# Two units per run: order of scores, queries, values and projections in an attention block with a gate

## The chip, the core and the metric

The kernel runs on one core of a Trainium2 chip. The metric is the device time of one execution in microseconds (us); lower is better. Five executions of the kernel before took 929.92, 929.92, 930.09, 930.19 and 933.02 us: median 930.09. A profile of one more execution shows where the time goes.

## The reference

```python
def _A_ref(x, k_cache, v_cache, wq, wo):          # 32 heads of 192, 2048 rows
    W = min(4096, max(256, Sk // 4))              # 512: the last 512 keys
    q = (x @ wq) split into heads
    k, v = k_cache[:, :, Sk - W:, :], v_cache[:, :, Sk - W:, :]
    p = softmax(q @ k^T * Dh ** -0.5)
    return (p @ v) joined over heads @ wo

def _B_ref(x, w_gate, w_up, w_down):
    return (sigmoid(x @ w_gate) * (x @ w_up)) @ w_down

xn = layernorm(x)                                  # x: 2048 x 640, bf16
out = x + _A_ref(xn, ...) * silu(_B_ref(xn, ...))
```

The sizes: 2048 rows, width 640, 32 heads with 192 values each, 512 keys per head, 1536 hidden columns in the gated part. Everything comes in and goes out as bf16.

## The kernel before

Two stages follow each other. **Stage one** normalizes x, turns it so that the width lies on the partitions (`xnT`), and computes the gated part into `gate`, in four blocks of 512 rows. Weights come in pieces, issued at lines 158 to 171, mostly on SyncE's queue (SP), the first of the gate weights on ScalarE's (ACT). Row block 0 starts tile by tile (`tile_gates`, L291); the first matmuls need the first weights and the first tiles of x. During block 2 the first group of attention inputs is loaded (L344), during block 3 its keys are turned (L346). At the end the queries of unit 0 are computed with 128-row matmuls (`query_psum`, L358).

**Stage two** is attention and its output projection. Heads come in 8 groups of 4, rows in 4 blocks of 512; one group on one block is a **unit**, 32 in all, numbered u = 4 x group + block. A unit has four kinds of work on TensorE (PE):

- `scores` (L390): eight steps, one for each of two head pairs and four key chunks. A head has 192 columns, cut as 3 x 64, so a step is 6 matmuls of 64 rows, two of them side by side in the two halves of the array, into the two halves of one PSUM bank pair. ScalarE takes the Exp of the 128 x 1024 result (L394) into the tile `E`.
- `queries` for the next unit (L408): six half-steps of 10 matmuls, also of 64 rows, set between the score steps, so that PE has work while ScalarE does the Exp. VectorE (DVE) copies the first element of a half-done sum (L413) and the finished sum (L415).
- `values` (L425): four heads, each 16 matmuls of 128 rows and 193 columns (the last column is the softmax sum); DVE takes the reciprocal and divides (L430, L431) into `o_st`.
- `project` (L445): for each of four row tiles, 12 matmuls of 128 rows of the unit before, added to `acc` by DVE (L458, L460), and written out in the last group (L449 to L456). In group 6 of 0 to 7, GpSimd (POOL) multiplies `acc` by the gate and adds the row of x (L463 to L465).

The loop at line 467 does, for each unit, first its scores with the queries of unit u + 1, and then its values with the projections of unit u - 1. The order on every engine is the order of the program: the scheduling is manual. PSUM is used as four bank pairs, `bank[0]` to `bank[3]`; the numbers in the calls pick one.

The inputs of a group: `wq_sb` (query weights), `k_st` (keys as loaded), `k_perm` (keys permuted by four POOL copies, L112), `kT` (keys turned by eight DMA transposes on SP, L128), `vbuf` (values, four loads), `wo_sb` (output weights). `wq_sb`, `kT`, `vbuf` and `wo_sb` have two buffers each. `load_group` and `load_wo` for the next group are called after the scores of block 1 and issue on POOL's queue; `turn_keys` after those of block 2. After a unit's values, `turn_out` (L437) turns `o_st` into `oT` with four DMA transposes on SP. The last unit has an order of its own (lines 491 to 504).

Of the kernel before, what the change touches and what calls it, by code (L numbers as in the profile page):

```python
# [15 lines left out]
def kernel(  # L16
# [13 lines left out]
    nc = tc.nc  # L30
# [31 lines left out]
    psum = ctx.enter_context(tc.tile_pool(name="psum", bufs=1, space=bass.MemoryType.PSUM))  # L62
    rs = dict(side="right")
    pers = ctx.enter_context(tc.tile_pool(name="pers", bufs=1, **rs))
    load2 = ctx.enter_context(tc.tile_pool(name="load2", bufs=2, **rs))
    load1 = ctx.enter_context(tc.tile_pool(name="load1", bufs=1, **rs))
    qpool = ctx.enter_context(tc.tile_pool(name="qpool", bufs=2, **rs))


    bank = [psum.tile([P, 2, 512], F32, name=f"bank{i}") for i in range(4)]  # L70
# [9 lines left out]

    xnT = pers.tile([P, NB, NCD, TB], BF16, name="xnT")
    gate = pers.tile([P, NT, D], BF16, name="gate")
    vbuf = [pers.tile([P, 4, KC, VP], BF16, name=f"vbuf{i}") for i in range(2)]

    wq_r = A_wq.rearrange("(c p) n -> p c n", p=P)
    wo_r = A_wo.rearrange("(c p) d -> p c d", p=P)
# [3 lines left out]

    grp = {}

    def load_group(g, eng):

        d = grp.setdefault(g, {})
        d["wq"] = load2.tile([P, NCD, GW], BF16, name="wq_sb")
        eng.dma_start(d["wq"][:], wq_r[:, :, g * GW:(g + 1) * GW])
        kst = load1.tile([P, 4, KC, DH], BF16, name="k_st")
        kv = slice(Sk - W, Sk)
        eng.dma_start(  # L100
            kst[:].rearrange("p h j d -> p h (j d)"),
            A_k_cache[0, 4 * g:4 * g + 4, kv, :].rearrange("h (p j) d -> p h (j d)", j=KC),
        )
        d["v"] = vbuf[g % 2]
        for h in range(4):
            eng.dma_start(  # L106
                d["v"][:, h, :, 0:DH],
                A_v_cache[0, 4 * g + h, kv, :].rearrange("(p j) d -> p j d", j=KC),
            )
        kp = load1.tile([P, 2, KC, DJ, P], BF16, name="k_perm")  # L110
        for h in range(4):
            nc.gpsimd.tensor_copy(  # L112
                kp[:, h // 2, :, :, (h % 2) * H2:(h % 2) * H2 + H2],
                kst[:, h, :, :].rearrange("p c (i j) -> p c j i", j=DJ),
            )
        d["kp"] = kp

    def load_wo(g):
        d = grp[g]
        d["wo"] = wo_pool.tile([P, GC, D], BF16, name="wo_sb")  # L120
        nc.gpsimd.dma_start(d["wo"][:], wo_r[:, g * GC:(g + 1) * GC, :])

    def turn_keys(g):
        d = grp[g]
        d["kT"] = load2.tile([P, 2, DJ, W], BF16, name="kT")
        for pr in range(2):
            for c in range(KC):
                nc.sync.dma_start_transpose(  # L128
                    d["kT"][:, pr, :, c * P:(c + 1) * P],
                    d["kp"][:, pr, c, :, :].rearrange("p j i -> p (j i)"),  # L130
                )


    with ExitStack() as bctx:
# [18 lines left out]
        def load_f(eng, w, r, f0, f1, c0=0, c1=NCD):  # L153
            eng.dma_start(w[:, c0:c1, f0 * P:f1 * P], r[:, c0:c1, f0 * P:f1 * P])
# [3 lines left out]
        nc.vector.memset(wg_sb[:, 0, 0:2], 0.0)  # L158
        load_x(0, 1)
        load_x(1, 1)  # L160
        load_f(nc.scalar, wg_sb, wg_r, 0, 4)
        load_f(nc.sync, wu_sb, wu_r, 0, 4, 0, 3)
        load_x(2, 1)
        load_f(nc.sync, wu_sb, wu_r, 0, 4, 3, NCD)
        load_x(3, 1)
# [7 lines left out]
        nc.scalar.activation(junk[:], eps_t[:], AF.Sqrt)  # L173
        nc.gpsimd.memset(mhalf[:], -0.5)
        make_identity(nc, ident[:])
        for i in range(2):
            nc.gpsimd.memset(vbuf[i][:, :, :, DH:DH + 2], 1.0)

        def dummy(n):
            for _ in range(n):  # L180
# [150 lines left out]
        for b in range(1, NB):  # L331
            for f in range(2):
                gated(b, f, k)
                k = (k + 1) % 4
            for q in range(TQ):
                down(b - 1, q, k)
                k = (k + 1) % 4
            if b == 1:
                load_x(3 * TQ, TQ)
            for f in range(2, NF):  # L340
                gated(b, f, k, norm_piece(b + 1, f - 4) if b + 1 < NB and f >= 4 else None)
                k = (k + 1) % 4
            if b == 2:
                load_group(0, nc.sync)  # L344
            if b == 3:
                turn_keys(0)  # L346
        for q in range(TQ):
# [4 lines left out]
        def query_psum(u, n, k, half):  # L352

            g, b = u // NB, u % NB
            wq = grp[g]["wq"]
            col = (n // DJ) * 2 * DH + n % DJ
            for c in range(NCD):
                nc.tensor.matmul(bank[k][:, half, :], lhsT=wq[:, c, col:col + DJ * (P - 1) + 1:DJ],  # L358
                                 rhs=xnT[:, b, c, :], start=(c == 0), stop=(c == NCD - 1))

        qT[0] = qpool.tile([P, 2 * DJ, TB], BF16, name="qT")
        for m in range(DJ):
            for half in range(2):
                query_psum(0, 2 * m + half, k, half)
            nc.vector.tensor_copy(qT[0][:, 2 * m:2 * m + 2, :], bank[k][:])
            k = (k + 1) % 4


    wo_pool = ctx.enter_context(tc.tile_pool(name="wo_pool", bufs=2))
    acc_pool = ctx.enter_context(tc.tile_pool(name="acc_pool", bufs=1))  # L370
    e_pool = ctx.enter_context(tc.tile_pool(name="e_pool", bufs=2))
    o_pool = ctx.enter_context(tc.tile_pool(name="o_pool", bufs=1))
    oT_pool = ctx.enter_context(tc.tile_pool(name="oT_pool", bufs=2))
    small = ctx.enter_context(tc.tile_pool(name="small", bufs=4))
    fin = ctx.enter_context(tc.tile_pool(name="fin", bufs=4))

    acc = acc_pool.tile([P, NT, D], F32, name="acc")
    NU = NG * NB
# [17 lines left out]
    def queries(u, m, k, second):  # L396

        g, b = u // NB, u % NB
        wq = grp[g]["wq"]
        if u not in qT:  # L400
            qT[u] = qpool.tile([P, 2 * DJ, TB], BF16, name="qT")
        for c in range(NCD):
            for i in range(2):
                half = i ^ second
                n = 2 * m + half
                col = (n // DJ) * 2 * DH + n % DJ
                r = slice(i * H2, (i + 1) * H2)
                nc.tensor.matmul(bank[k][:, half, :], lhsT=wq[r, c, col:col + DJ * (P - 1) + 1:DJ],  # L408
                                 rhs=xnT[r, b, c, :], start=(c == 0 and not second),
                                 stop=(c == NCD - 1), skip_group_check=bool(second))  # L410
        if not second:

            nc.vector.tensor_copy(seen[:, m, :], bank[k][:, :, 0])  # L413
        else:
            nc.vector.tensor_copy(qT[u][:, 2 * m:2 * m + 2, :], bank[k][:])  # L415
# [1 line left out]
    o_st = {}  # L417

    def values(u, h, k):
        g = u // NB  # L420
        v, e = grp[g]["v"], E[u, h // 2]
        o4 = wide(k).rearrange("p (q n) -> p q n", q=TQ)
        for q in range(TQ):
            for c in range(KC):
                nc.tensor.matmul(o4[:, q, 0:DH + 1], lhsT=e[:, c, h % 2, q * P:(q + 1) * P],  # L425
                                 rhs=v[:, h, c, 0:DH + 1], start=(c == 0), stop=(c == KC - 1))
        if h == 0:
            o_st[u] = o_pool.tile([P, TQ, GW], BF16, name="o_st")
        rden = small.tile([P, TQ, 1], F32, name="rden")
        nc.vector.reciprocal(rden[:], o4[:, :, DH:DH + 1])  # L430
        nc.vector.tensor_tensor(o_st[u][:, :, h * DH:(h + 1) * DH], o4[:, :, 0:DH],  # L431
                                rden[:].to_broadcast([P, TQ, DH]), ALU.mult)
# [31 lines left out]
            nc.gpsimd.tensor_tensor(acc[:, t, :], acc[:, t, :], gate[:, t, :], ALU.mult)  # L464
            nc.gpsimd.tensor_tensor(acc[:, t, :], acc[:, t, :], x_sb[:], ALU.add)  # L465

    for u in range(NU):
        g, b = u // NB, u % NB
        nxt = u + 1 < NU
        sc = [(pr, c) for pr in range(2) for c in range(KC)]  # L470
        if nxt:
            for i, what in enumerate(((0, 0), (1, 0), (0, 1), (1, 1), (2, 0), None, (2, 1), None)):
                scores(u, *sc[i], i % 2)
                if what is not None:
                    queries(u + 1, what[0], 2 + what[0] % 2, what[1])
        if b == 1 and g + 1 < NG:
            load_group(g + 1, nc.gpsimd)
            load_wo(g + 1)
        if b == 2 and g + 1 < NG:
            turn_keys(g + 1)  # L480
        if nxt:
            order = (3, 2, 0, 1, 3, 2, 0, 1) if u else (3, None, 2, None, 0, None, 1, None)
            for q in range(4):
                values(u, q, order[2 * q])
                if q == 3:
                    turn_out(u)
                if u > 0:
                    project(u - 1, q, order[2 * q + 1], nc.sync)


    u = NU - 1
    for i, k in enumerate((3, 2, 0, 1, 3, 2)):
        scores(u, *sc[i], k)
    project(u - 1, 0, 0, nc.sync)
    scores(u, *sc[6], 1)
    scores(u, *sc[7], 3)
    for h, k in enumerate((2, 0, 1, 3)):
        values(u, h, k)
    turn_out(u)
    for q, k in ((1, 2), (2, 0), (3, 1)):  # L500
        project(u - 1, q, k, nc.sync)
    for q, k in ((0, 3), (1, 2), (2, 0)):
        project(u, q, k, nc.scalar)
    project(u, 3, 1, None)


# [28 lines left out]
```

The softmax here doesn't subtract the row's maximum and nothing guards it: scores larger than these inputs give would overflow.

## Time and profile before

| what | us |
|---|---|
| median of five executions | 930.09 |
| the profiled execution | 930.21 |
| its span in the profile | 928.4 |
| PE busy | 916.9 |
| VectorE busy | 467.6 |
| ScalarE busy | 304.8 |
| POOL busy | 126.5 |
| first score matmul / last unit's first score matmul | 170.57 / 899.49 |
| from one unit to the next, in the steady part | 23.72 |

The times inside the profile count from the start of the span. The span is 1.8 us shorter than the time of the same execution. "PE" is the matmuls, "PEld" the loading of their stationary operands, which overlaps. A line such as L390 is that line of the kernel before. In a timeline, square brackets behind an entry give how long the engine stood idle before it, and what ended that. In the list of DMA issues the columns are the tensor, the queue and kind, the count, the size of one and the median time from issue to landing. The TensorE clock was granted in full nearly throughout (mean 0.999).

### The profile page before, as it was taken

To read this page: it belongs to the slowest core of one execution; us is meant where nothing else is said; L and a number is where in the kernel's file an instruction comes from. 1 tells how busy PE (TensorE), PEld (TensorE's weight loads), DVE (VectorE), ACT (ScalarE), POOL (GpSimd) and SP (SyncE) were. 2 spreads that over 40 slices of the span, in tenths; PEclk is the share of its full clock that TensorE was granted. 3 is DMA by queue.
4 is the path that set the end of the run, shared out by engine and by line. 5 is a ranking of instruction groups with operands and counts; after the bars stand their busy time and mean duration, and the time that the engine had idled before them with its cause. 6 is when DMAs were issued, how large, how long until landed. Compare 5 with 4: busy or idle time off the path is not lost.

```text
span 928.4 us, 18032 instructions
## 1 busy us (share of the span) xinstructions
PE 916.9 (99%) x7954; PEld 545.4 (59%) x8034; DVE 467.6 (50%) x739; ACT 304.8 (33%) x333; POOL 126.5 (14%) x154
## 2 busy tenths in 40 slices
PE   8999999999999999999999999999999999999997
PEld 6445455565666556666556666556666666666665
DVE  5452522455545545445545445544555555445657
ACT  4222222433333333333333333333333333333341
POOL 1000100400010001000200020002000205555000
PEclk9999999999999999999999999999999999999999
DMA  9310420616224423443343433263326234422223
GB/s 320 78 29 1 128 46 1 196 36 145 53 53 78 121 68 61 77 95 94 61 77 62 118 70 78 57 124 69 78 49 131 69 69 76 93 63 64 50 67 102
DMA packets 157823, 76.69 MB, mean 83 GB/s; under 512 B 140800, under 2 KB 151664, under 8 KB 157744
## 3 DMA queue, kind: packets, MB, share of 16 engines
q1 hardware_dynamic: 149264, 45.90, 24.8%
q0 software_dynamic: 7248, 28.38, 10.9%
q8 instruction: 63, 1.03, 0.5%
q10 hardware_dynamic: 1232, 1.25, 0.4%
q14 instruction: 16, 0.13, 0.1%
HBM read 39.45 MB, written 2.62 MB: 45 GB/s over the span
## 4 chain that ended last, share of the span: by engine, by line
PE 97%; DVE 1%; DMA 1%; issue 1%; SPq 0%; ACT 0%; DVEq 0%
PE bank L408 22%; PE bank L445 21%; PE bank L425 19%; PE bank L390 18%; PE bank L241 10%; PE bank L253 6%; PE bank L291 1%; PE bank L358 1%; DMA x_sb<-in_A_x_dram 1%; DVE gate L454 1%; DVE o_sb L449 1%; PE bank L221 0%; SPq L149 0%; ACT xnT L227 0%; DVE st L189 0%
## 5 line engine op out<-in xcount | busy, mean ns | idle before, releaser
L394 ACT ACTIVATE E<-bank 128x1024 bf16<-128x1024 f32 x256 | 257.9, 1023 | 477.4 <-PE bank L390 465.6
L408 PE MATMUL bank<-xnT,wq_sb 64*128 64x512 bf16 x1860 | 231.3, 376 | 0.0
L445 PE MATMUL bank<-wo_sb,oT 128*128 128x128 bf16 (+1 forms) x1473 | 225.2, 296 | 3.3
L390 PE MATMUL bank<-qT,kT 64*128 64x512 bf16 x1536 | 202.1, 376 | 0.0
L425 PE MATMUL bank<-vbuf,E 128*128 128x193 bf16 x2048 | 191.0, 247 | 0.0
L425 PEld LDWEIGHTS <-E 128*128 128x128 bf16 x2048 | 167.8, 98 | 24.2 <-issue 13.6
L415 DVE CAST qT<-bank 128x1024 bf16<-128x1024 f32 x93 | 113.9, 1225 | 132.8 <-PE bank L408 132.8
L445 PEld LDWEIGHTS <-oT 128*128 128x128 bf16 x1536 | 121.3, 98 | 76.6 <-issue 0.4
L408 PEld LDWEIGHTS <-wq_sb 64*128 64x128 bf16 x1860 | 97.0, 100 | 104.8
L390 PEld LDWEIGHTS <-kT 64*128 64x128 bf16 x1536 | 72.9, 94 | 90.1 <-issue 8.8
L431 DVE TENSOR_TENSOR o_st<-bank,rden 128x768 bf16<-128x768 f32 x128 | 122.5, 957 | 4.8 <-DVE rden L430 0.4
L460 DVE TENSOR_TENSOR acc<-bank,acc 128x640 f32<-128x640 f32 x96 | 79.2, 825 | 44.1 <-PE bank L445 44.1
L413 DVE COPY seen<-bank 128x2 f32<-128x2 f32 x93 | 14.8, 159 | 93.9 <-PE bank L408 93.8
L430 DVE RECIPROCAL rden<-bank 128x4 f32<-128x4 f32 x128 | 23.3, 182 | 71.0 <-PE bank L425 70.8
L241 PE MATMUL bank<-xnT,wg_sb 128*128 128x512 bf16 x216 | 54.5, 379 | 0.2
L241 PE MATMUL bank<-xnT,wu_sb 128*128 128x512 bf16 x215 | 54.4, 379 | 0.3
L253 PE MATMUL bank<-wd_sb,hT 128*128 128x128 bf16 (+1 forms) x376 | 52.4, 297 | 0.4
L247 DVE TENSOR_TENSOR hT<-bank,sig 128x512 bf16<-128x512 f32 x44 | 30.3, 689 | 42.9 <-ACT sig L244 42.9
L244 ACT ACTIVATE sig<-bank 128x512 bf16<-128x512 f32 x44 | 26.3, 597 | 68.4 <-PE bank L241 65.3
L106 POOL DMA_DIRECT2D vbuf<-in_A_v_cache_dram x28 | 20.9, 747 | 184.9 <-PE bank L425 184.9
L253 PEld LDWEIGHTS <-hT 128*128 128x128 bf16 x384 | 29.7, 98 | 23.1
L241 PEld LDWEIGHTS <-wu_sb 128*128 128x128 bf16 x220 | 21.5, 98 | 26.0
(51 smaller groups left out, 275.8 us busy)
## 6 DMA issues: line engine op xcount, KB each, us to landing
wo_sb<-in_A_wo_dram POOLq DMA_DIRECT2D x8, 960.0 KB, 7.4
wq_sb<-in_A_wq_dram POOLq DMA_DIRECT2D x7, 960.0 KB, 6.3
k_st<-in_A_k_cache_dram POOLq DMA_DIRECT2D x7, 768.0 KB, 8.3
vbuf<-in_A_v_cache_dram POOLq DMA_DIRECT2D x28, 192.0 KB, 3.0
row<-in_A_x_dram POOLq DMA_DIRECT2D x16, 160.0 KB, 2.7
oT<-o_st SPq DMA_TRANSPOSE x128, 2.6
x_sb<-in_A_x_dram SPq DMA_DIRECT2D x3, 640.0 KB, 10.3
wd_sb<-in_B_w_down_dram SPq DMA_DIRECT2D x1, 1920.0 KB, 13.8
```

Source lines behind the costliest of these rows:

```text
L241: nc.tensor.matmul(bank[k][:, half, 0:r1 - r0], lhsT=w[:, c, f * P:(f + 1) * P], rhs=xnT[:, b, c, r0:r1], start=(c == 0), stop=(c == NCD - 1))
L244: nc.scalar.activation(sig[:, 0:r1 - r0], bank[k][:, 0, 0:r1 - r0], AF.Sigmoid)
L247: nc.vector.tensor_tensor(hT[b][:, f, r0:r1], bank[k][:, 1, 0:r1 - r0], sig[:, 0:r1 - r0], ALU.mult)
L253: nc.tensor.matmul(wide(k)[:, d0:d1], lhsT=hT[b][:, f, q * P:(q + 1) * P], rhs=wd_sb[:, f, d0:d1], start=(f == 0), stop=(f == NF - 1))
L390: nc.tensor.matmul(bank[k][:, i, :], lhsT=kT[r, pr, j, c * P:(c + 1) * P], rhs=q[r, pr * DJ + j, :], start=(j == 0), stop=(j == DJ - 1))
L394: nc.scalar.activation(E[u, pr][:, c, :, :], bank[k][:], AF.Exp, scale=scale_qk)
L408: nc.tensor.matmul(bank[k][:, half, :], lhsT=wq[r, c, col:col + DJ * (P - 1) + 1:DJ], rhs=xnT[r, b, c, :], start=(c == 0 and not second), ...
L415: nc.vector.tensor_copy(qT[u][:, 2 * m:2 * m + 2, :], bank[k][:])
L425: nc.tensor.matmul(o4[:, q, 0:DH + 1], lhsT=e[:, c, h % 2, q * P:(q + 1) * P], rhs=v[:, h, c, 0:DH + 1], start=(c == 0), stop=(c == KC - 1))
L431: nc.vector.tensor_tensor(o_st[u][:, :, h * DH:(h + 1) * DH], o4[:, :, 0:DH], rden[:].to_broadcast([P, TQ, DH]), ALU.mult)
L445: nc.tensor.matmul(wide(k)[:, d0:d1], lhsT=oT[u][:, cc, q * P:(q + 1) * P], rhs=wo[:, cc, d0:d1], start=(cc == 0), stop=(cc == GC - 1))
L460: nc.vector.tensor_tensor(acc[:, t, :], wide(k)[:, 0:D], acc[:, t, :], ALU.add)
```

## The change

The order of stage two is changed from one unit at a time to two. The loop goes over pairs (u0, u0 + 1): the scores of both units come first, with the queries of u0 + 2 and u0 + 3 between them; then the values of both, with the projections of u0 - 2 and u0 - 1. The last pair has an order of its own: 16 score steps with the eight projections of the pair before among them, then the values of both units, then their projections. Unit 1's queries are computed ahead of the loop, with unit 0's.

The buffers of a group become single: one each for `wq_sb`, `kT`, `vbuf` and `wo_sb`. In their place there are four `qT`, four `E`, and two `o_st`; the rows of x at the end get two buffers instead of four. The keys are loaded in two halves through one `k_st` of half the size, with two POOL copies after each. The output weights of the last group go into the place of the query weights, and all output weights are issued on SP instead of POOL. The calls that load and turn move to the first point at which the single buffer is free: query weights and keys after the scores of the first pair of a group, the turn of the keys after the scores of the second pair, values after that pair's values, output weights after the values and projections of the next group's first pair.

At the very start the first gate weights are cut in two, three of five chunks on ACT and two on SP, and the first three chunks of the up weights move from SP to ACT.

The core of the diff:

```diff
-    load2 = ctx.enter_context(tc.tile_pool(name="load2", bufs=2, **rs))
     load1 = ctx.enter_context(tc.tile_pool(name="load1", bufs=1, **rs))
-    qpool = ctx.enter_context(tc.tile_pool(name="qpool", bufs=2, **rs))
+    qpool = ctx.enter_context(tc.tile_pool(name="qpool", bufs=4, **rs))
...
-    vbuf = [pers.tile([P, 4, KC, VP], BF16, name=f"vbuf{i}") for i in range(2)]
+    vbuf = pers.tile([P, 4, KC, VP], BF16, name="vbuf")
...
+    def load_keys(g, eng):
+        kp = load1.tile([P, 2, KC, DJ, P], BF16, name="k_perm")
+        for pr in range(2):
+            kst = load1.tile([P, 2, KC, DH], BF16, name="k_st")
+            h0 = 4 * g + 2 * pr
+            eng.dma_start(
+                kst[:].rearrange("p h j d -> p h (j d)"),
+                A_k_cache[0, h0:h0 + 2, kv, :].rearrange("h (p j) d -> p h (j d)", j=KC),
+            )
+            for i in range(2):
+                nc.gpsimd.tensor_copy(
+                    kp[:, pr, :, :, i * H2:(i + 1) * H2],
+                    kst[:, i, :, :].rearrange("p c (i j) -> p c j i", j=DJ),
+                )
...
     def load_wo(g):
         d = grp[g]
-        d["wo"] = wo_pool.tile([P, GC, D], BF16, name="wo_sb")
-        nc.gpsimd.dma_start(d["wo"][:], wo_r[:, g * GC:(g + 1) * GC, :])
+        if g < NG - 1:
+            d["wo"] = wo_pool.tile([P, GC, D], BF16, name="wo_sb")
+        else:
+            d["wo"] = load1.tile([P, GC, D], BF16, name="wo_last", tag="wq_sb")
+        nc.sync.dma_start(d["wo"][:], wo_r[:, g * GC:(g + 1) * GC, :])
...
-        load_f(nc.scalar, wg_sb, wg_r, 0, 4)
-        load_f(nc.sync, wu_sb, wu_r, 0, 4, 0, 3)
+        load_f(nc.scalar, wg_sb, wg_r, 0, 4, 0, 3)
+        load_f(nc.sync, wg_sb, wg_r, 0, 4, 3, NCD)
+        load_f(nc.scalar, wu_sb, wu_r, 0, 4, 0, 3)
...
+        ks = iter((1, 2, 3, 0, 3, 1))
+        for u in range(2):
+            qT[u] = qpool.tile([P, 2 * DJ, TB], BF16, name="qT")
+            for m in range(DJ):
+                k = next(ks)
+                for half in range(2):
+                    query_psum(u, 2 * m + half, k, half)
+                nc.vector.tensor_copy(qT[u][:, 2 * m:2 * m + 2, :], bank[k][:])
...
+    order = (2, 3, 0, 1)
+    for u0 in range(0, NU - 2, 2):
+        g, second = u0 // NB, u0 % NB != 0
+        more = g + 1 < NG
+        for u in (u0, u0 + 1):
             for i, what in enumerate(((0, 0), (1, 0), (0, 1), (1, 1), (2, 0), None, (2, 1), None)):
                 scores(u, *sc[i], i % 2)
                 if what is not None:
-                    queries(u + 1, what[0], 2 + what[0] % 2, what[1])
+                    queries(u + 2, what[0], 2 + (what[0] + u) % 2, what[1])
+        if more and not second:
+            load_wq(g + 1, nc.gpsimd)
+            load_keys(g + 1, nc.gpsimd)
+        if more and second:
+            turn_keys(g + 1)
+        if not more:
+            load_wo(g)
+        for u in (u0, u0 + 1):
             for q in range(4):
+                if u0 > 0:
+                    values(u, q, order[2 * q % 4])
+                    project(u - 2, q, order[(2 * q + 1) % 4], nc.sync)
+                else:
+                    values(u, q, order[q])
+            turn_out(u)
+        if more and second:
+            load_values(g + 1, nc.gpsimd)
+        if 0 < g < NG - 1 and not second:
+            load_wo(g)
+
+    u = NU - 2
+    sc = [(v, *s) for v in (u, u + 1) for s in sc]
+    for i in range(6):
+        scores(*sc[i], order[i % 4])
+    for q in range(2):
+        project(u - 2, q, q, nc.sync)
+    for i in range(6, 12):
+        scores(*sc[i], order[(i - 6) % 4])
+    for q in range(2, 4):
+        project(u - 2, q, q - 2, nc.sync)
+    for i in range(12, 16):
+        scores(*sc[i], order[i % 4])
+    for q in range(4):
+        project(u - 1, q, order[q], nc.sync)
+    for v in (u, u + 1):
+        for h in range(4):
+            values(v, h, order[h])
+        turn_out(v)
+    for q in range(4):
+        project(u, q, order[q], nc.sync)
+    for q in range(4):
+        project(u + 1, q, order[q], nc.scalar if q < 3 else None)
```

More of the change, by code (lines that the diff above doesn't have):

```diff
@@ L91, with load_wq @@
     grp = {}
-    def load_group(g, eng):
+    kv = slice(Sk - W, Sk)
+    def load_wq(g, eng):
         d = grp.setdefault(g, {})
-        d["wq"] = load2.tile([P, NCD, GW], BF16, name="wq_sb")
+        d["wq"] = load1.tile([P, NCD, GW], BF16, name="wq_sb")
         eng.dma_start(d["wq"][:], wq_r[:, :, g * GW:(g + 1) * GW])
[L98 to L104, printed above, removed]
+    def load_keys(g, eng):
[12 more added lines that the diff above has]
+                )
+        grp[g]["kp"] = kp
@@ L105, in load_group, with load_values @@
+    def load_values(g, eng):
         for h in range(4):
             eng.dma_start(
-                d["v"][:, h, :, 0:DH],
+                vbuf[:, h, :, 0:DH],
                 A_v_cache[0, 4 * g + h, kv, :].rearrange("(p j) d -> p j d", j=KC),
             )
[L110 to L115, printed above, removed]
@@ L116, in load_group @@
-        d["kp"] = kp
     def load_wo(g):
         d = grp[g]
-        d["wo"] = wo_pool.tile([P, GC, D], BF16, name="wo_sb")
-        nc.gpsimd.dma_start(d["wo"][:], wo_r[:, g * GC:(g + 1) * GC, :])
+        if g < NG - 1:
[3 more added lines that the diff above has]
+        nc.sync.dma_start(d["wo"][:], wo_r[:, g * GC:(g + 1) * GC, :])
     def turn_keys(g):
         d = grp[g]
-        d["kT"] = load2.tile([P, 2, DJ, W], BF16, name="kT")
+        d["kT"] = load1.tile([P, 2, DJ, W], BF16, name="kT")
@@ L175 @@
         make_identity(nc, ident[:])
-        for i in range(2):
-            nc.gpsimd.memset(vbuf[i][:, :, :, DH:DH + 2], 1.0)
+        nc.gpsimd.memset(vbuf[:, :, :, DH:DH + 2], 1.0)
         def dummy(n):
@@ L343 @@
             if b == 2:
-                load_group(0, nc.sync)
+                load_wq(0, nc.sync)
+                load_keys(0, nc.sync)
+                load_values(0, nc.sync)
             if b == 3:
@@ L359, in query_psum @@
                                  rhs=xnT[:, b, c, :], start=(c == 0), stop=(c == NCD - 1))
[L361 to L369, printed above, removed]
+        ks = iter((1, 2, 3, 0, 3, 1))
[6 more added lines that the diff above has]
+                nc.vector.tensor_copy(qT[u][:, 2 * m:2 * m + 2, :], bank[k][:])
+    wo_pool = ctx.enter_context(tc.tile_pool(name="wo_pool", bufs=1))
     acc_pool = ctx.enter_context(tc.tile_pool(name="acc_pool", bufs=1))
-    e_pool = ctx.enter_context(tc.tile_pool(name="e_pool", bufs=2))
-    o_pool = ctx.enter_context(tc.tile_pool(name="o_pool", bufs=1))
+    e_pool = ctx.enter_context(tc.tile_pool(name="e_pool", bufs=4))
+    o_pool = ctx.enter_context(tc.tile_pool(name="o_pool", bufs=2))
     oT_pool = ctx.enter_context(tc.tile_pool(name="oT_pool", bufs=2))
     small = ctx.enter_context(tc.tile_pool(name="small", bufs=4))
-    fin = ctx.enter_context(tc.tile_pool(name="fin", bufs=4))
+    fin = ctx.enter_context(tc.tile_pool(name="fin", bufs=2))
     acc = acc_pool.tile([P, NT, D], F32, name="acc")
@@ L419, in values @@
     def values(u, h, k):
-        g = u // NB
-        v, e = grp[g]["v"], E[u, h // 2]
+        e = E[u, h // 2]
         o4 = wide(k).rearrange("p (q n) -> p q n", q=TQ)
@@ L425, in values @@
                 nc.tensor.matmul(o4[:, q, 0:DH + 1], lhsT=e[:, c, h % 2, q * P:(q + 1) * P],
-                                 rhs=v[:, h, c, 0:DH + 1], start=(c == 0), stop=(c == KC - 1))
+                                 rhs=vbuf[:, h, c, 0:DH + 1], start=(c == 0), stop=(c == KC - 1))
         if h == 0:
@@ L465, in project @@
             nc.gpsimd.tensor_tensor(acc[:, t, :], acc[:, t, :], x_sb[:], ALU.add)
[L467 to L471, printed above, removed]
+    sc = [(pr, c) for pr in range(2) for c in range(KC)]
+    order = (2, 3, 0, 1)
[3 more added lines that the diff above has]
+        for u in (u0, u0 + 1):
             for i, what in enumerate(((0, 0), (1, 0), (0, 1), (1, 1), (2, 0), None, (2, 1), None)):
@@ L474 @@
                 if what is not None:
-                    queries(u + 1, what[0], 2 + what[0] % 2, what[1])
[L476 to L479, printed above, removed]
+                    queries(u + 2, what[0], 2 + (what[0] + u) % 2, what[1])
[3 more added lines that the diff above has]
+        if more and second:
             turn_keys(g + 1)
-        if nxt:
-            order = (3, 2, 0, 1, 3, 2, 0, 1) if u else (3, None, 2, None, 0, None, 1, None)
+        if not more:
+            load_wo(g)
@@ L483 @@
+        for u in (u0, u0 + 1):
             for q in range(4):
[L484 to L504, printed above, removed]
+                if u0 > 0:
[6 more added lines that the diff above has]
+            load_values(g + 1, nc.gpsimd)
```

## The prediction

> **What bounds the kernel.** I read the page's busy table first, then the chain that ended last, then the timeline of one unit in the steady part, and last the waits and the DMA issues.
>
> ```profile
> span 928.4 us, 18032 instructions
> ...
> PE 916.9 (99%) x7954; PEld 545.4 (59%) x8034; DVE 467.6 (50%) x739; ACT 304.8 (33%) x333; POOL 126.5 (14%) x154
> ...
> PE 97%; DVE 1%; DMA 1%; issue 1%; SPq 0%; ACT 0%; DVEq 0%
> ```
>
> PE sets the time: 99% busy and 97% of the chain, with no wait behind it. A transfer or an engine that already hides can give nothing. Only PE's own work, or a gap inside it, can. So I took one unit from the timeline between 500 and 560 us (columns: start, duration, engine, line, operation).
>
> ```profile
> 518.20 1.79 PE L445 MATMUL bank<-wo_sb,oT 128*128 128x512 bf16 x12
> ...
> 519.92 0.33 PEld L390 LDWEIGHTS <-kT 64*128 64x128 bf16 x6 [0.26 <-issue]
> 519.93 0.82 PE L390 MATMUL bank<-qT,kT 64*128 64x512 bf16 x6
> ...
> 528.57 1.46 PE L390 MATMUL bank<-qT,kT 64*128 64x512 bf16 x12
> ...
> 529.42 1.94 ACT L394 ACTIVATE E<-bank 128x1024 bf16<-128x1024 f32 x2 [0.64 <-PE bank L390]
> ...
> 529.87 1.24 PE L408 MATMUL bank<-xnT,wq_sb 64*128 64x512 bf16 x10
> ...
> 530.94 0.81 PE L390 MATMUL bank<-qT,kT 64*128 64x512 bf16 x6
> ...
> 531.68 1.28 PEld L425 LDWEIGHTS <-E 128*128 128x128 bf16 x16 [0.42 <-issue]
> 531.69 1.51 PE L425 MATMUL bank<-vbuf,E 128*128 128x193 bf16 x16
> ```
>
> Starts, not durations, tell the pace, since the matmuls overlap. A score step takes (529.87 - 528.57)/2 = 0.65 us inside the run of two, a query half-step 1.07 (529.87 to 530.94). But the last score step, 530.94 to 531.69, takes 0.75: 0.10 is lost where PE goes from 64-row matmuls to 128-row ones. At the other end a projection takes 1.63 between its neighbours (509.31 to 510.94 in the same view), so 518.20 should end at 519.83, and the next scores start at 519.93: 0.10 to 0.11 lost. The weight loads show it too: both "issue" gaps stand at these two places and nowhere else in the unit. The total agrees: 8 x 0.65 + 6 x 1.07 + 4 x (1.33 + 1.63) = 23.5, and units repeat every 23.72 us.
>
> **Part 1, switches removed.** Before, PE enters the 64-row matmuls 33 times (32 units, and once more in the tail) and leaves them 33 times: 66 switches. After, there are 15 pairs in the loop and 3 runs of scores in the tail: 18 entries and 18 exits, 36 switches. So 15 of each kind go: 15 x 0.10 + 15 x 0.11 = **3.15 us**. It is all on PE's path, so it counts in full. Everything else that PE does stays: scores, values and projections are the same in number; unit 1's queries become 30 matmuls of 128 rows in place of 60 of 64, which take 164.00 to 170.57 us for unit 0 now, 6.5 us, against 6 x 1.07 = 6.4: nothing.
>
> The Trainium skill, "TensorEngine Tiling (Array Packing)", Key Properties, says that changing the tiling mode drains TensorE, which fits the place of the gaps. "TensorE: Matmul & The Clock Gate", Single matmul latency, puts the part of a lone matmul that isn't streaming at 398 cycles of 2.4 GHz, 166 ns; were all of that exposed, 30 switches would be an estimated 5.0 us and the time about 925.0. The row has 0.10 to 0.11, and I go by the row.
>
> **Part 2, the new seams.** Inside a run, unit u+1's first score step follows unit u's last. It writes bank 0, whose last reader is the Exp of step 6. Taking the rows above: the two Exps end at 529.42 + 1.94 = 531.36, and the new step would start at 530.94 + 0.65 = 531.59. Margin 0.23 us; the shortest hand-over to PE in the trace is 0.06 (xn ends at 8.53, PE starts at 8.59), so 0.17 is left and I take zero. If the cover were gone by 0.1, it would cost 15 x 0.1 = 1.5 us. The next step uses bank 1: it starts 1.72 later, at 533.3, and Exp 7 ends at about 532.8. The query banks alternate with the unit, so the last cast (to 532.38) isn't waited for. On the values side values and projection alternate as now, DVE needs 0.18 + 0.96 + 0.82 of each 2.96 us, and four banks rotate. Below zero: the first unit's values without projections end once instead of once per unit; that is 0.1 us at most.
>
> **Part 3, single buffers and moved loads.** A scores run is now 2 x 11.65 = 23.3 us, a values run 23.7 (10.7 in the first pair, 8 x 1.33, which has no projections). Each load has to fit between the last reader and the first user.
>
> ```profile
> wq_sb<-in_A_wq_dram POOLq DMA_DIRECT2D x7, 960.0 KB, 6.3
> k_st<-in_A_k_cache_dram POOLq DMA_DIRECT2D x7, 768.0 KB, 8.3
> ...
> oT<-o_st SPq DMA_TRANSPOSE x128, 2.6
> ...
> kT<-k_perm SPq DMA_TRANSPOSE x64, 2.4
> ```
>
> (The last column is us from issue to landing.)
> - Query weights: free at the end of the scores run, wanted 23.7 + 0.65 us later; they need 0.87 + 6.3, at most 7.4. In the first pair the window is 10.7 + 0.65 = 11.3 against 8.3: the tightest, 3 us of cover, once.
> - Keys: two half loads with POOL's copies between, 2 x (0.78 + 8.2 + 2 x 0.83) = 21.3 us, wanted by SP's transposes 34 us later at the earliest.
> - kT: SP may turn the next keys only after the scores run and has the values run, 23.7 us. Eight turns took 10.5 to 11.8 us and 2.4 to land: 14.2. Cover 9.5 us. The output turns queued behind them on SP are wanted a whole scores run later.
> - Values: issued on POOL after the values run, 4 x 0.75 + 3.1 (at most 8.6) against 23.3. In group 7 they stand behind eight rounds of POOL's work on acc, now without a pause of a scores run between; a round took about 4.0 us (776.39 to 780.41), so these end some 36 us after the values run begins, the four loads by 42 to 48, and they are wanted from 47 on, one each 2.96 us. I take zero; the bad end costs 1 us.
> - Output weights, moved from POOL to SP: four output turns 5.2, issue, 7.4 to 8.6 to land, 14 of 24.6 us. The key turns behind them wait for the same scores run anyway. The last ones, in the query weights' place, come a values run ahead.
> All nothing on the path. The skill's front page, "Trainium Kernel Development and Optimization", Best Practices, asks to double-buffer, so that transfers overlap with compute, which speaks against single buffers. Were no transfer overlapped, the eight key turns alone would be an estimated 7 x 14.2 = 99 us more; by the rows the other phase's run covers them, and I go by the rows.
>
> **Part 4, start and tail.** In the first microseconds PE waits for a chain that begins at the third row block of x:
>
> ```profile
> 7.69 0.49 DVE L189 BATCH_NORM_STATS2 st<-x_sb 128x6 f32<-128x320 bf16 x1 [0.89 <-DMA x_sb<-in_A_x_dram]
> ...
> 8.59 0.45 PE L221 MATMUL bank<-ident,xn 128*128 128x128 bf16 x5 [0.48 <-DVE xn L209]
> ```
>
> Now 704 KB stand ahead of it on SP and 640 KB on ACT; after, 576 and 768. If the two queues share evenly, 1472 KB must have moved instead of 1504: 0.1 us earlier at the page's first-slice 320 GB/s. Bounds: PE's wait of 0.48 gone, or the up weights, which move behind on ACT, late by the same: -0.5 to +0.4. I take -0.1. ACT's second issue, 0.46, lies ahead of a square root that waits 1.10 for DVE.
> The tail interleaves 16 score steps with 8 projections, 6 / 2 / 6 / 2 / 4 / 4, then 8 values and 8 projections: 10.4 + 26.1 + 10.7 us of PE. Exp at 0.95 each (7.62 for eight) is slower than 0.65, but each stretch of projections (3.3 us) lets it catch up, as the present tail does once (903.48). The last output turns begin some 5 us before their projections. Nothing.
>
> **Sum.** The profiled execution took 930.21 (span 928.4 and 1.8 around it): 930.21 - 3.15 - 0.1 = 926.96. It lies 0.12 above the median of 930.09, so **926.8 us**.
>
> **Rivals.**
> - Only half of the gap is the switch: the rest belongs to something that a seam keeps (a wait for Exp or PSUM at each of 15 seams, 0.1 each). For it: the margin of 0.17 is small. Against it: runs of score steps and of projections in the trace show no loss. 926.8 + 1.5 = 928.3, from 927.6 to 930.
> - Slower: kT in one buffer. Place: SP's eight turns between two scores runs, seven times. It decides once a turn takes more than (23.7 - 2.4)/8 = 2.66 us; at the longest kT turn in the trace, 2.99, all eight land 26.3 us after, 2.6 late x 7 = 18 us: 945. Against it: the median is 1.25. It needs 5 us in all, 0.73 a group, to be slower by 0.2%.
> - A larger gain: the start gives 0.5 and the switches hide more than the starts show (0.14 each): 925.5.
>
> **Chances.** The forecast, 926.0 to 927.6: 0.78. Seams: 0.12. Slower: 0.05. Larger gain: 0.05. The range takes the start's ends and the seams' 1.5: 925.7 to 928.7. A measurement of this kernel can tell about 0.2% (1.9 us) from no change. Faster by more than that is all of the forecast, the larger gain and a few hundredths of the seams less what I keep for errors in them: 0.84; within it 0.10; slower 0.06.
>
> **What would show it.** PE's busy time should fall by about 3 us, units come in pairs 47.2 us apart (23.72 x 2 - 0.21), and the "issue" gaps of 0.42 and 0.26 halve in number; between two units' scores the step should stay at 0.65. Wrong would be: a PE wait for kT, wq_sb, vbuf or wo_sb in the list of waits, Exp named ahead of a unit's first score step, or a start of the first scores far from 170.6 + 6.5.

## The result, and the profile after

The changed kernel takes **928.24 us** (median of 21 runs, 927.27 to 928.9), the kernel before 930.13 (median of 39 runs, 929.82 to 933.02). The ratio is 0.9977 with a 95% interval of 0.9971 to 0.9983, so the change saves 1.9 us (0.2%), where 3.3 were forecast. The profiled execution of the changed kernel took 928.24, with a span of 926.5 us; before it was 930.21 and 928.4.

In the lines of the changed kernel, scores are L403, queries L421, values L437, projections L457, the gate matmuls of the start L300 and the turn of a normalized tile L230. Its page answers to the three lines that the prediction began with:

```profile
span 926.5 us, 17964 instructions
...
PE 915.0 (99%) x7925; PEld 546.9 (59%) x8004; DVE 469.0 (51%) x736; ACT 302.8 (33%) x333; POOL 125.7 (14%) x152
...
PE 96%; DVE 1%; DMA 1%; issue 1%; SPq 0%; DVEq 0%; ACT 0%
```

PE still sets the time. Its 915.0 us of busy time can't be held against the 916.9 of before, since matmul records are missing in both (7925 of 8004 here, 7954 of 8034 there).

The timeline of one pair in the steady part is where the forecast can be read (start, duration, engine, line, operation):

```profile
519.04 1.28 PEld L437 LDWEIGHTS <-E 128*128 128x128 bf16 x16 [0.42 <-issue]
519.05 1.51 PE L437 MATMUL bank<-vbuf,E 128*128 128x193 bf16 x16
...
542.86 0.33 PEld L403 LDWEIGHTS <-kT 64*128 64x128 bf16 x6 [0.27 <-issue]
...
553.88 1.46 PE L403 MATMUL bank<-qT,kT 64*128 64x512 bf16 x12
...
555.17 1.24 PE L421 MATMUL bank<-xnT,wq_sb 64*128 64x512 bf16 x10
...
566.27 1.28 PEld L437 LDWEIGHTS <-E 128*128 128x128 bf16 x16 [0.42 <-issue]
566.28 1.51 PE L437 MATMUL bank<-vbuf,E 128*128 128x193 bf16 x16
```

From one run of values to the next is 566.28 - 519.05 = 47.23 us, where two units of before took 2 x 23.72 = 47.44: 0.21 saved a pair. Every later pair of the loop takes 47.22 to 47.24. The 12 matmuls at 553.88 are the last score step of one unit and the first of the next: (555.17 - 553.88)/2 = 0.645 a step, so the seam costs nothing.

The list of waits (engine and line, what it waited for: total us, times, longest) shows the same, and one thing more. Before:

```profile
PEld L425 <- issue: 13.6, 32, 0.4
...
PEld L390 <- issue: 8.8, 33, 0.4
...
PEld L445 <- issue: 0.4, 1, 0.4
...
PEld L291 <- DMA wg_sb<-in_B_w_gate_dram: 0.4, 1, 0.4
```

and after:

```profile
PEld L437 <- issue: 6.4, 15, 0.4
...
PEld L403 <- issue: 4.8, 18, 0.4
...
PEld L457 <- issue: 1.3, 3, 0.4
...
PEld L300 <- DMA wg_sb<-in_B_w_gate_dram: 0.7, 1, 0.7
```

There are 18 gaps where PE goes over to the 64-row matmuls and 15 + 3 where it comes back: 36 switches, where before had 33 and 32 + 1, that is 66. No wait of PE for `kT`, `wq_sb`, `vbuf` or `wo_sb` is in the list. The last line has grown: at the start the weight loads of PE wait for gate weights, 0.7 us instead of 0.4, and now its matmuls stand idle for them too. The timeline of the first microseconds shows this and what followed:

```profile
7.76 0.62 PE L300 MATMUL bank<-xnT,wg_sb 128*128 128x128 bf16 x8 [0.54 <-DMA wg_sb<-in_B_w_gate_dram]
...
8.71 0.49 DVE L198 BATCH_NORM_STATS2 st<-x_sb 128x6 f32<-128x320 bf16 x1 [1.67 <-DMA x_sb<-in_A_x_dram]
...
9.60 0.45 PE L230 MATMUL bank<-ident,xn 128*128 128x128 bf16 x5 [0.34 <-DVE xn L218]
...
10.63 1.28 PE L300 MATMUL bank<-xnT,wg_sb 128*128 128x128 bf16 x20
```

The third block of x is there at 8.7 us instead of 7.7, tile 1 is turned at 9.60 instead of 8.59, and the gate matmuls of tile 1 start at 10.63 instead of 9.62. This is the line of before:

```profile
9.62 1.28 PE L291 MATMUL bank<-xnT,wg_sb 128*128 128x128 bf16 x20
```

The up weights are late as well: the first matmuls with them start at 8.42 instead of 7.26.

The first scores start at 178.06 instead of 170.57: 6.48 for the queries of unit 1, which moved there, and 1.01 that is lost. The tail has the second loss:

```profile
904.20 5.13 SPq L449 DMA_TRANSPOSE oT<-o_st  x3
...
908.42 0.93 PE L457 MATMUL bank<-wo_last,oT 128*128 128x512 bf16 x4 [0.18 <-DMA oT<-o_st]
```

SP issues the first output turn of the last pair at 904.20, it lands 4.2 us later, and PE's matmuls stand idle for 0.18 us before the last projections.

The spans add up: -3.15 for 15 pairs at 0.21, +1.01 at the start, and +0.24 left over, of which 0.18 is this idle time and 0.06 the queries of unit 1 (6.48 against 6 x 1.07 in the loop), make -1.9, and 928.4 - 926.5 is 1.9.

### The profile page after: what moved, and what is told of

It reads as the page before. It is cut to its first block, busy times and chain, and to the rows that moved or that the text cites. A ratio compares the mean times of both kernels' runs of the same rounds, so it can differ in the third digit from the quotient of the medians.

```text
span 926.5 us, 17964 instructions
## 1 busy us (share of the span) xinstructions
PE 915.0 (99%) x7925; PEld 546.9 (59%) x8004; DVE 469.0 (51%) x736; ACT 302.8 (33%) x333; POOL 125.7 (14%) x152
## 4 chain that ended last, share of the span: by engine, by line
PE 96%; DVE 1%; DMA 1%; issue 1%; SPq 0%; DVEq 0%; ACT 0%
PE bank L457 21%; PE bank L421 21%; PE bank L437 18%; PE bank L403 18%; PE bank L250 10%; PE bank L262 6%; PE bank L369 1%; PE bank L300 1%; DMA x_sb<-in_A_x_dram 1%; DVE gate L466 1%; DVE o_sb L461 1%; DMA oT<-o_st 0%; PE bank L230 0%; SPq L158 0%; ACT xnT L236 0%
## 5 line engine op out<-in xcount | busy, mean ns | idle before, releaser
L421 PE MATMUL bank<-xnT,wq_sb 64*128 64x512 bf16 x1800 | 223.7, 376 | 0.0
L457 PE MATMUL bank<-wo_sb,oT 128*128 128x512 bf16 (+1 forms) x1288 | 197.9, 296 | 3.0
L403 PE MATMUL bank<-qT,kT 64*128 64x512 bf16 x1536 | 198.4, 376 | 0.0
L437 PE MATMUL bank<-vbuf,E 128*128 128x193 bf16 x2048 | 189.5, 247 | 0.0
L437 PEld LDWEIGHTS <-E 128*128 128x128 bf16 x2048 | 168.6, 98 | 18.0 <-issue 6.4
L428 DVE CAST qT<-bank 128x1024 bf16<-128x1024 f32 x90 | 110.2, 1225 | 128.5 <-PE bank L421 128.5
L457 PEld LDWEIGHTS <-oT 128*128 128x128 bf16 x1536 | 121.0, 98 | 78.6 <-issue 1.3
L421 PEld LDWEIGHTS <-wq_sb 64*128 64x128 bf16 x1800 | 93.0, 100 | 102.3
L403 PEld LDWEIGHTS <-kT 64*128 64x128 bf16 x1536 | 74.0, 94 | 89.8 <-issue 4.8
```

What stands on the lines that cost most here:

```text
L403: nc.tensor.matmul(bank[k][:, i, :], lhsT=kT[r, pr, j, c * P:(c + 1) * P], rhs=q[r, pr * DJ + j, :], start=(j == 0), stop=(j == DJ - 1))
L457: nc.tensor.matmul(wide(k)[:, d0:d1], lhsT=oT[u][:, cc, q * P:(q + 1) * P], rhs=wo[:, cc, d0:d1], start=(cc == 0), stop=(cc == GC - 1))
```

## The experiments

The theory after the result: the switches give what was forecast, and the new order of the first loads takes 1.0 us of it back. The rivals: the start is not the cause, or it is the cut of the gate weights and not the moved up weights; and the gap at a switch is not what the switch costs.

**e1_old_start: the changed kernel with the loads at the start as before.**

```diff
-        load_f(nc.scalar, wg_sb, wg_r, 0, 4, 0, 3)
-        load_f(nc.sync, wg_sb, wg_r, 0, 4, 3, NCD)
-        load_f(nc.scalar, wu_sb, wu_r, 0, 4, 0, 3)
+        load_f(nc.scalar, wg_sb, wg_r, 0, 4)
+        load_f(nc.sync, wu_sb, wu_r, 0, 4, 0, 3)
```

> The changed kernel with the start loads of the kernel before (gate weights whole on ACT, up weights on SP); all else as changed. Theory A (the start alone took back 1.0 us of the switches' 3.15): the first full run of tile 1's gate matmuls starts at 9.6 us again instead of 10.63, and the time is 928.24 - 1.0 = 927.2 us, with less spread than the 927.3 to 928.9 of the changed kernel. Rival B (the missing gain lies at the seams or in the tail, the start costs nothing): 928.2 us. Rival C (the start moves, but a later wait swallows it): first matmuls at 9.6 and still 928.2.

Measured: 927.39 us (926.75 to 927.91), ratio to before 0.9968 (0.9956 to 0.9981), 0.85 less than the changed kernel. Tile 1's gate matmuls start at 9.46, 1.17 earlier. Not all of that arrives, since the first output turn of the last pair, issued at 903.02, takes 4.4 us to land instead of 4.2, and PE waits longer for it (its timeline):

```profile
907.49 13.21 PE L456 MATMUL bank<-wo_last,oT 128*128 128x512 bf16 x96 [0.42 <-DMA oT<-o_st]
```

0.42 instead of 0.18: 1.17 - 0.24 = 0.93, and the spans differ by 0.9 (926.5 and 925.6). So the start is the cause of the missing 1.0 us.

**e2_new_start_only: the kernel before with the new loads at the start,** that is e1's edit in reverse, on the other kernel.

> The kernel before with only the changed start loads. Theory A: 930.1 + 1.0 = 931.1 us, and the first score matmul 1.0 us later than 170.57. Rival B: 930.1 us.

Measured: 930.84 (930.09 to 932.03), ratio 1.0006 (0.9997 to 1.0015): 0.78 more than the 930.06 of before, measured beside it, but the interval of the ratio holds 1, so the time alone tells nothing. The profile is clearer: tile 1's gate matmuls at 10.42 instead of 9.62, the first scores at 171.37 instead of 170.57, 0.80 each. The loss is there without the new order of stage two.

**e3_more_switches: the kernel before with 124 switches more.** Two of the six query half-steps of a unit (31 units have them in the loop) are done with five matmuls of 128 rows in place of ten of 64, each between score steps of 64 rows. The work is the same, and each of the 62 half-steps adds a switch in and one out.

```diff
-        for c in range(NCD):
+        if m == 2:
+            n = 2 * m + second
+            col = (n // DJ) * 2 * DH + n % DJ
+            for c in range(NCD):
+                nc.tensor.matmul(bank[k][:, second, :], lhsT=wq[:, c, col:col + DJ * (P - 1) + 1:DJ],
+                                 rhs=xnT[:, b, c, :], start=(c == 0), stop=(c == NCD - 1))
+        for c in range(NCD if m < 2 else 0):
...
-            nc.vector.tensor_copy(seen[:, m, :], bank[k][:, :, 0])
+            nc.vector.tensor_copy(seen[:, m, :], bank[k][:, 0, 0:2] if m == 2 else bank[k][:, :, 0])
```

> The kernel before, in which the last two of the six query half-steps of each unit are five 128-row matmuls each in place of ten 64-row ones: the same streaming time, no new wait, but 4 more switches in each of 31 units, 124 in all. If a switch costs what the gaps in the trace show (0.105 us): 930.1 + 13.0 = 943.1 us. If the whole of a lone matmul's latency is exposed (0.166 us, from the Trainium skill's page on TensorE): an estimated 950.7. Rival (the gaps belong to the change of phase, not to the change of rows): 930.1 us.

Measured: 944.02 (two runs, 943.68 and 944.35), ratio 1.0148 (1.0129 to 1.0166): 13.96 more than the 930.06 of before, and 13.96 / 124 = 0.113 us a switch. A unit in the steady part takes 24.16 us (values start at 515.04 and 539.20) instead of 23.72, which makes 0.11. Its timeline has the same gaps at the new places:

```profile
534.65 0.77 PEld L406 LDWEIGHTS <-wq_sb 128*128 128x128 bf16 x5 [0.42 <-issue]
534.65 1.26 PE L406 MATMUL bank<-xnT,wq_sb 128*128 128x512 bf16 x5
...
535.84 0.98 PEld L390 LDWEIGHTS <-kT 64*128 64x128 bf16 x12 [0.42 <-issue]
535.85 1.47 PE L390 MATMUL bank<-qT,kT 64*128 64x512 bf16 x12
```

The half-step now takes 535.85 - 534.65 = 1.20 instead of 1.07. Each gap of the weight loads lasts 0.42 us, but only 0.113 of it is lost: the "issue" idle time of PEld is no price.

The Trainium skill, "TensorEngine Tiling (Array Packing)", Key Properties, says that a change of the tiling mode drains TensorE, without a price. A loss at each change of rows fits that, and these runs put it at 0.11; the 166 ns of a lone matmul, from "TensorE: Matmul & The Clock Gate", Single matmul latency, would have made an estimated 124 x 0.166 = 20.6 us, and 13.96 were measured.

**e4_old_start_tail: e1 with another order in the tail.** Unit 30's values come in the middle of unit 29's projections, so that its output turns have unit 31's values and two projections as cover.

```diff
-    for q in range(4):
+    for q in range(2):
...
-    for v in (u, u + 1):
-        for h in range(4):
-            values(v, h, order[h])
-        turn_out(v)
+    for h in range(4):
+        values(u, h, order[(h + 2) % 4])
+    turn_out(u)
+    for q in range(2, 4):
+        project(u - 1, q, order[q], nc.sync)
+    for h in range(4):
+        values(u + 1, h, order[h])
+    turn_out(u + 1)
```

> As the first of these, and in the tail the values of unit 30 come between the second and the third projection of unit 29, so that the output turns of unit 30 begin 3 us earlier. Theory A with the tail's wait of 0.18 us for oT: 927.2 - 0.2 = 927.0 us, and no wait for oT in the list. Rival: the wait is replaced by one for PSUM or DVE, 927.2.

Measured: 926.84 (926.67 to 927.51), ratio 0.9964 (0.9952 to 0.9977), 0.55 less than e1; the ranges overlap, but the profiles agree with it: e4's tile 1 starts at 9.66, 0.20 later than e1's, and its span is 0.4 shorter (925.2 and 925.6). PE waits for no `oT` any more. The median lies below those of both kernels. In this tail the turns land after a median of 2.6 us; one of them, the last of unit 30, takes 4.1, and PE does not wait for it.

**e5_gate_cut_only and e6_up_on_act_only: which half of the new start?** e5 is the changed kernel with the up weights back on SP; the cut of the gate weights stays.

```diff
-        load_f(nc.scalar, wu_sb, wu_r, 0, 4, 0, 3)
+        load_f(nc.sync, wu_sb, wu_r, 0, 4, 0, 3)
```

> The changed kernel, in which the first up weights stay on SP, so that only the cut of the gate weights (three chunks on ACT, two on SP) is left of the changed start. The measure is the start of tile 1's gate matmuls: 10.63 us in the changed kernel, 9.46 and 9.66 with the old start. Theory A1 (the up weights on ACT delay x's third block): about 9.6, and 927.3 us. Theory A2 (the cut does it): about 10.6, and 928.2.

e6 is the changed kernel with the gate weights whole on ACT, and the up weights behind them there.

```diff
-        load_f(nc.scalar, wg_sb, wg_r, 0, 4, 0, 3)
-        load_f(nc.sync, wg_sb, wg_r, 0, 4, 3, NCD)
+        load_f(nc.scalar, wg_sb, wg_r, 0, 4)
```

> The changed kernel with the gate weights whole on ACT again and the up weights behind them on ACT, so that only the move of the up weights is left of the changed start. Theory A1: tile 1's gate matmuls start at about 10.6 us, 928.2 us. Theory A2: about 9.6, 927.3. If the third block of x, which now has only 320 KB ahead of it on SP, decides by itself, it lands earlier and the matmuls wait for the up weights instead: about 9.6 again.

Measured: e5 927.29 (926.86 to 927.71), ratio 0.9969 (0.9958 to 0.9981), tile 1's gate matmuls at 9.52. So the cut alone is harmless, and the up weights, moved to ACT behind it, are what costs. e6 took 927.48 (926.58 to 928.33), ratio 0.9971 (0.996 to 0.9982), tile 1 at 10.17. Its profiled execution is the 928.33 one, at the upper end of its runs, and shows the last of the expectation's outcomes, though not at its 9.6. The third block of x, nothing but two blocks of x ahead of it on SP, comes early, and PE waits for the up weights instead (timeline of e6):

```profile
6.74 0.48 DVE L197 BATCH_NORM_STATS2 st<-x_sb 128x6 f32<-128x320 bf16 x1
...
8.46 0.84 PE L299 MATMUL bank<-xnT,wu_sb 128*128 128x128 bf16 x12 [0.95 <-DMA wu_sb<-in_B_w_up_dram]
```

The late up weights alone cost this profile some 0.5 us (10.17 against 9.62 of before). So in the changed kernel, where both are late, an earlier third block of x would have won back only about half of the 1.01. The median of e6 does not show the loss: it is within 0.2 of e1 and e5, with runs from 926.58 to 928.33.

**e7_norm_first and e8_norm_first_again: can VectorE's order at the start give more?** e4 with tile 1 normalized ahead of the first statistics of tile 2.

```diff
-        stats_half(2, 0)
         normal(1)
+        stats_half(2, 0)
```

> Old start loads, the changed tail order (926.84 us), and on VectorE the normalization of tile 1 ahead of the statistics of tile 2, so that it no longer stands behind the landing of x's third block. If the chain at the start runs through that order: PE's turn of tile 1 starts at about 8.0 to 8.1 us instead of 8.6, and up to 0.5 us goes, 926.4. Rival (the weights or tile 2 are late next): no gain, 926.8.

Measured: 926.54 (926.36 to 929.3), ratio 0.9961 (0.9947 to 0.9975). The profiled execution is the one of 929.3, in which the gate weights landed late and tile 1's gate matmuls started at 11.99, so nothing could be read on the edit. It was run again, with e4 beside it on the same chip:

> The kernel of e7_norm_first once more, since its profiled execution was its slowest and said nothing on the edit; the e4_old_start_tail kernel runs beside it. If VectorE's order is what keeps TensorE waiting ahead of the turn of tile 1 (a wait of 0.47 us in e1_old_start), tile 1's gate matmuls start at 9.0 to 9.3 us instead of 9.5 to 9.7, and the median lies 0.3 us below that of e4_old_start_tail, about 926.5. If the landing of x's third block or of the weights decides instead, the start stays at 9.5 to 9.7 and the medians agree within 0.15.

> The kernel of e4_old_start_tail unchanged, on the same chip as e8_norm_first_again, as its measure: 926.8, first score matmuls at about 176.9 to 177.1 us, no TensorE wait for oT in the tail.

Measured: e8 926.72 (926.55 to 926.97), ratio 0.996 (0.9947 to 0.9974), and e9, which is e4 unchanged, 926.71 (926.53 to 927.13), ratio 0.9962 (0.9949 to 0.9974). The medians agree within 0.01. Tile 1's gate matmuls start at 9.62 in e8, after a wait of 0.77 for the gate weights, and at 9.35 in e9, which has no such wait: the landing of the first loads decides. PE does not wait for VectorE ahead of the turn of tile 1 in e8, where the late weights would have hidden such a wait in either order. In e9, with the old order, the weight loads there still wait 0.32 for it. So the two runs show no gain, but not that the order has nothing to give when the weights are early.

## Why the prediction was right in kind and wrong in size

**Part 1, the switches: right.** 0.21 a pair, 15 times, as worked out from the starts. e3 confirms the price from the other side: 0.113 against 0.10 to 0.11. The busy time of PE falls as said when all records are there: 917.7 to 919.2 in the seven runs of the new order with all 8004 (e1 and e4 to e9) against 922.0 in e2, which has the old order and all 8034: 2.8 to 4.3 less, forecast about 3.

**Part 2, the seams: right.** The step across the seam is 0.645. The measured 928.24 lies next to the 928.3 of the rival "seams", and yet that rival is refuted: its 1.5 us would have to be in the pairs, and these take 47.23.

**Part 3, the single buffers: right.** No wait of PE for any of the four tensors. The least certain place was group 7's values. They were issued from 839.85 to 842.87, landed at most 5.3 us later, so by 848.2, and PE came to the first of them at 849.65. The slower rival, a late `kT`, did not occur: eight key turns at 519.18 took 10.6 us of SP, forecast 10.5 to 11.8.

**Part 4, the start: this term failed.** It said "If the two queues share evenly, 1472 KB must have moved instead of 1504: 0.1 us earlier", with -0.5 to +0.4 as bounds. It was +1.01, outside them. The sum of bytes itself came out nearly so. If a queue's packets go in order, the third block of x ends 864 KB into SP's queue before (704 + 160), at 0.88 MB, and 736 KB into it after, at 0.75 MB. SP's queue had moved that much by 6.6 us before, when the two queues together had moved about 1500 KB, and by 6.9 after, with about 1460. Two other things were wrong. First, the bytes came more slowly: by 6 us the two queues together had moved 1.32 MB before and 1.19 MB after, so the mark came 0.3 later, where the arithmetic said 0.1 earlier. These are the queues in the microsecond from 4 to 5, SP's being q1 and ACT's q10, of before:

```profile
q10 hardware_dynamic: 374, 0.38, 107.0%
q1 hardware_dynamic: 7, 0.01, 2.0%
```

and of after (packets, MB, share):

```profile
q10 hardware_dynamic: 252, 0.24, 70.5%
q1 hardware_dynamic: 105, 0.11, 40.6%
```

Before, ACT's load had the engines nearly to itself from 4 to 5 us and was through by 6 (656 packets); SP then moved 349 packets from 6 to 7 us, with none of ACT's beside it. After, ACT's queue still has the up weights and moves 133 from 6 to 7, and SP 202. Why fewer bytes had moved by then, the runs don't settle.

Second, bytes moved are not a landing, and this is the larger part. Counted from the point at which SP's queue had moved enough, the block landed 1.1 us later before and 1.8 in the changed kernel (1.7 in e2, 0.5 to 1.4 in the other eight runs). The trace shows where the lag sits. The semaphore that reports a load goes up in 16 steps, as many as there are DMA engines, and the last step is the landing. Before, the 16 steps of the third block of x came from 6.90 to 7.67 us. After, 13 of them came from 7.09 to 7.59, and the last three at 7.92, 8.27 and 8.68; in e2, 14 came by 7.46 and the last two at 8.41 and 8.47. The middle of the steps is only 0.2 us later after than before, and the rest of the 1.01 is a few steps that lag. The loads beside it have the same kind of tail: the up weights on ACT end with 7.69, 7.95, 8.22 and 8.37, after twelve steps by 7.12. So, if each step stands for one engine, a few of the 16 engines were behind with both queues' loads. What held these few back stays open.

The Trainium skill, "DMA: Bandwidth & Descriptors", Queues, rings and completion order, says that each DMA engine goes round-robin, packet by packet, between the queues that it has work for. The microsecond from 4 to 5 in e5 agrees with it (187 packets of q1, 181 of q10). Before's 7 against 374 don't look so, though SP's load had been issued at 1.67; whether its packets had reached the engines by then, the trace does not show.

**Part 4, the tail: a small miss.** "The last output turns begin some 5 us before their projections. Nothing." They began some 4 us before (904.20, and PE wanted them at 908.0 to 908.2), and the first one landed after 4.2 us, where the median of all turns is 2.6. That cost 0.2 and, in e1, e5 and e6, where it landed after 4.4 to 4.6 us, 0.4 to 0.6. Here too 15 of its 16 steps came in good time, by 906.71, and the last at 908.37. A turn that lands late is not rare: the changed kernel has 14 of 128 that took 4.4 us or more. The term was put at nothing against the median row of 2.6 us, with too little room for such a turn. e4 shows that the order of the tail can hide it. Why the last step lags stays open.

In the sum: forecast -3.25, measured -1.9; 1.11 of the 1.35 between them is the start, 0.24 the tail and the queries of unit 1. With the old start and the other tail (e4, e9) the kernel is at 926.8 and 926.7. That is the forecast's number, but it was reached with another start and another tail than the forecast's.

That the 928.24 still lies within the stated 925.7 to 928.7 is in part luck: most of the room that the range had above was for the seams, which cost nothing, and the start and the tail used it.

## What to carry to other kernels

Count the switches between row modes on TensorE and price them by the loss between the starts of neighbouring steps, not by the idle time of the weight loads: here putting equal work together paid the 0.105 us a switch that the starts had shown, and single buffers were enough where the other phase's run was longer than the load. A change to the first loads should be costed by when each load lands, tensor by tensor, not by bytes ahead of it; here a second load on the other queue, with a piece of weights ahead of the block on its own, went with a delay of a microsecond for a small one. And where a measured total agrees with a rival, look for that rival's mark in the trace before believing it.

## What the runs showed that was not expected

- The landing of one small load lagged its queue's own byte count by 0.5 to 1.4 us in nine runs and by 1.7 to 1.8 in two others, and there two or three of its 16 steps came about a microsecond after the others.
- The first loads move by themselves: with the same loads at the start, tile 1's gate matmuls began at 9.35 to 9.66 in five runs (before, e1, e4, e8, e9), at 10.09 in e3, and at 11.99 in e7, whose time was 929.3 where the other four runs of that kernel took 926.36 to 927.0. In e7 15 of the 16 steps of the first gate weights had come by 6.01 us, and the last came at 7.58.
- The first DMA turn of the tail landed after 4.2 us in the changed kernel and 4.4 in e1, where the median of the turns in e4's tail is 2.6.
